# The first two h tiles of the second expert, computed together and copied by token thirds

## The chip, the cores and the metric

The kernel runs on one core of a Trainium2 chip. The metric is device time in microseconds of one execution. The core has a matrix engine (TensorE, PE in the profile, with its weight loads shown apart as PEld), three engines for elementwise work (VectorE = DVE, ScalarE = ACT, GpSimd = POOL) and queues that start transfers between HBM and SBUF, here all from SyncE (SP). PE writes its results to PSUM, from where DVE and ACT read them.

## What is computed

Three blocks follow each other on 1152 tokens (2 x 576) with a model width of 512: attention with rotary positions over 8 heads of 64, a first expert (x wa * x wb) wo of inner width 1536, and a second expert of inner width 2048. The change lies at the start of the second expert:

```python
def _moe2_ref(x, w_in, w_out):
    h = x @ w_in
    g = h - np.tanh(h)
    return (g @ w_out).astype(np.float32)
```

## The kernel before

Every operand of a matmul is split into a high and a low part in a reduced float32 format. `mm3` (lines 188 to 190) makes one product as three matmuls: high x high, high x low, low x high. The tokens are taken in thirds (`t`, TP = 384 columns); the model width in four chunks of 128 (`c`).

The first expert ends with the y units (line 714). For each token third t and each chunk d of the width, PE makes a y tile in PSUM, DVE adds it to yacc (L727), ACT copies the high part of the sum to yt[0] (L735), and POOL subtracts it from the sum for the low part yt[1] (L736). So yt is made chunk by chunk, the last token third last.

The second expert makes 16 h tiles, each of 128 inner columns and all 1152 tokens. `h_unit` (line 781) runs 36 matmuls per tile: 3 thirds x 4 chunks x 3, on the high and low parts of yt. A tile takes three banks of PSUM. There are two pools of one such buffer each: even tiles share one, odd tiles the other, so that tile f + 2 has to wait until the last reader of tile f is done. The odd pool and the pools of the o tiles lie where the last y tiles lay.

Then comes g = h - tanh(h), with a series for small h, on 128 x 1152 elements at a time (the last tile by thirds). ACT makes the square of h (L803), a square with a bias (L806), a mask (L807), tanh (L812) and at the end the high part of g (L818). DVE makes two products (L808, L813), the subtraction h - tanh (L816), a predicated copy that picks one of the two (L817), and the low part of g (L819). The readers of h are L803 and L812 on ACT and L813 and L816 on DVE. For the first two tiles ACT first copies h to the SBUF tile hs (L798); there DVE reads hs, while ACT still reads PSUM. Work buffers are tmpa for even tiles and tmpb for odd ones.

The o units (line 827) multiply g by w2, 12 matmuls for four h tiles and 128 tokens; they begin when the first g tiles are there. Between units, pieces of the weight conversion (lines 120 to 158: a DMA to st, then ACT and DVE steps) are put in with `cv`.

The order on each engine is fixed when the kernel is built: a scheduler lists the instructions of each engine, by the order in the code and by when it expects inputs. At run time each engine goes through its own list in order and waits for counters of the other engines. In the order rows below such a wait stands in brackets with the engine that is waited for; numbers in names are those of buffers.

Of the kernel before, what the change touches and what calls it, by code (L numbers as in the profile page):

```python
# [11 lines left out]
F32 = mybir.dt.float32  # L12
# [6 lines left out]

SIGN_BIT = -2147483648  # L20

# h - tanh(h) = h * u * (1/3 - C1 * u + C2 * u * u), u = h * h, for |h| <= TSMALL
TSMALL = 0.25
C0 = 1.0 / 3.0
C1 = -0.13329779010819712
C2 = 0.052115944387372236
# [3 lines left out]
def attention_moe_kernel(  # L30
# [13 lines left out]
    nc = tc.nc  # L44
# [4 lines left out]
    P = 128  # L49
# [16 lines left out]
        return tc.high_priority(offset=o) if o else nullcontext()  # L66
    PAIRS = [(b, hp) for b in range(B) for hp in range(NPAIR)]

    # ------------------------------------------------------------ pools
    const = ctx.enter_context(tc.tile_pool(name="const", bufs=1))  # L70
    actp = ctx.enter_context(tc.tile_pool(name="actp", bufs=2))
    big = ctx.enter_context(tc.tile_pool(name="big", bufs=2))
# [2 lines left out]
    ident = const.tile([P, P], F32, name="ident")  # L75
    make_identity(nc, ident)

    # ------------------------------------------------------------ float64 weights -> two float32r parts
    units = []
    for f in range(NF1):  # L80
        units.append(("ab", f))
# [130 lines left out]
            r.append(ps)  # L212
        ab_ps[f, t] = r

    # ------------------------------------------------------------ attention
    with ExitStack() as actx:
        ap1 = actx.enter_context(tc.tile_pool(name="ap1", bufs=1))
        ap2 = actx.enter_context(tc.tile_pool(name="ap2", bufs=2))
# [461 lines left out]
        mctx.close()  # L680
        return

    # ------------------------------------------------------------ first expert pair: (x wa * x wb) wo
    slots = ctx.enter_context(tc.tile_pool(name="slots", bufs=12))
    cbuf["slots"] = slots
    wcap[0] = WC1
# [71 lines left out]
            tc.tile_pool(name="ps_or", bufs=1, space=bass.MemoryType.PSUM, side="right")  # L758
        )]

    # ------------------------------------------------------------ second expert: g(y wi) w2
    wcap[0] = WC2
    oacc = big.tile([P, NTT, DM], F32, tag="big", name="oacc")
    cst = const.tile([P, 2], F32, name="cst")
# [8 lines left out]
    with ExitStack():  # L773
        nc.vector.memset(cst[:, 0:1], al)
        nc.vector.memset(cst[:, 1:2], -TSMALL * TSMALL)
        gf = {}
        tmps = [tmpa] + [slots.tile([P, 2, NP3, TP], F32, tag="slot", name="tmpb") for _ in range(NT2 - 1)]
        tht = slots.tile([P, 2, NP3, TP], F32, tag="slot", name="tht") if TM == 0 else None
        hs = slots.tile([P, 2, NP3, TP], F32, tag="slot", name="hs") if NH else None

        def h_unit(f):
            wc = get_w(("i", f // 2)).rearrange("p s (c f) -> p s c f", c=KC)
            ps = ps_h[f % 2].tile([P, NP3, 512], F32, tag="h", name="h")
            o = (f % 2) * P
            for t in range(NP3):
                for c in range(KC):
                    mm3(
                        ps[:, t, 0:TP], lambda s: wc[:, s, c, o:o + P],
                        lambda s: yt[s][:, c, t * TP:(t + 1) * TP], c == 0, c == KC - 1,
                    )  # L790
            g = slots.tile([P, 2, NP3, TP], F32R, tag="slot", name="g")
            ta = tmps[f % NT2]
            last = f == NF2 - 1
            for t in (range(NP3) if last else (slice(0, NP3),)):
                h = ps[:, t, 0:TP]
                if HA <= f < NH:
                    hc = hs[:, f % 2, t]
                    nc.scalar.copy(out=hc, in_=h)  # L798
                else:
                    hc = h  # L800
                u, vv, mk = ta[:, 0, t], ta[:, 1, t], g[:, 0, t]
                th = u if TM else tht[:, f % 2, t]
                nc.scalar.activation(out=u, in_=h, func=AF.Square)  # L803
                if CO and not TM:
                    nc.scalar.activation(out=th, in_=h, func=AF.Tanh)
                nc.scalar.activation(out=vv, in_=u, func=AF.Square, bias=cst[:, 0:1])  # L806
                nc.scalar.activation(out=mk, in_=u, func=AF.Relu, bias=cst[:, 1:2])  # L807
                nc.vector.scalar_tensor_tensor(  # L808
                    out=vv, in0=vv, scalar=de, in1=u, op0=ALU.add, op1=ALU.mult
                )  # L810
                if TM or not CO:
                    nc.scalar.activation(out=th, in_=h, func=AF.Tanh)  # L812
                nc.vector.scalar_tensor_tensor(  # L813
                    out=vv, in0=vv, scalar=C2, in1=hc, op0=ALU.mult, op1=ALU.mult
                )
                nc.vector.tensor_tensor(out=th, in0=hc, in1=th, op=ALU.subtract)  # L816
                nc.vector.copy_predicated(vv, mk.bitcast(U32), th)  # L817
                nc.scalar.copy(out=g[:, 0, t], in_=vv)  # L818
                nc.vector.tensor_tensor(out=g[:, 1, t], in0=vv, in1=g[:, 0, t], op=ALU.subtract)  # L819
            gf[f] = g  # L820
            if f % 2 == 1:
                retire(("i", f // 2))

        GE = 4
        wide = []

        def o_unit(gi, i):
            last = gi == NF2 // GE - 1
            n = i if i < CM else (i - 1 if i > CM else NTT - 1)
            if last and n % 8 not in (3, 7):  # L830
                if n % 4 == 0:
                    wide.append(ps_h[n // 4 % 2].tile([P, NP3, 512], F32, tag="h", name="ow"))
                ps = wide[-1][:, n % 4]
            else:
                ps = ps_o[n // 4 % 2 if last else n % 2].tile([P, DM], F32, tag="o", name="o")
            for n in range(GE):
                f = gi * GE + n
                wc = get_w(("2", f // 2)).rearrange("p s (c d) -> p s c d", c=2)
                if i == CM and f % 2 == 1:
                    retire(("2", f // 2))  # L840
                g = gf[f].rearrange("p s a x -> p s (a x)")
                for m, (a, c) in enumerate(((0, 0), (0, 1), (1, 0))):
                    nc.tensor.matmul(  # L843
                        ps, g[:, a, i * P:(i + 1) * P], wc[:, c, f % 2],
                        start=(n == 0 and m == 0), stop=(n == GE - 1 and m == 2),
                    )
            o = oacc[:, i]
            if gi == 0:
                nc.scalar.copy(out=o, in_=ps)
            else:  # L850
                nc.vector.tensor_tensor(out=o, in0=o, in1=ps, op=ALU.add)
            if last:
                ov = out.rearrange("(b r c) d -> b c r d", b=B, c=CW)
                if i == CM:
                    nc.sync.dma_start(out=out.rearrange("(r c) d -> c r d", c=CW)[CM], in_=o)
                else:
                    for s in range(2):
                        nc.sync.dma_start(out=ov[i // 5, (i if i < CM else i - 5) + 5 * s], in_=o[64 * s:64 * s + 64])

        oq = []  # L860
        for f in range(NF2):
            h_unit(f)
            for _ in range(OE):
                if CHB:
                    cv(CHB)
                if oq:
                    o_unit(*oq.pop(0))
                cv(CH)
            if f % GE == GE - 1:
                oq += [(f // GE, i) for i in (0, 1, 2, 3, 5, 6, 7, 8, 4)]  # L870
            if f >= WG:
                wcap[0] = WCG
        while oq:
            o_unit(*oq.pop(0))
# [45 lines left out]
```

## Time and profile before

| | us |
|---|---|
| runs of the kernel before (3) | 632.22, 631.37, 632.19 |
| their median | 632.19 |
| span of the profiled execution | 632.1 |
| PE busy | 608.2 |
| DVE busy | 481.1 |
| ACT busy | 348.4 |
| POOL busy | 132.4 |

One execution was taken by the profiler, and all durations come from it. No time around its span is given apart from it: the span is the profiled execution's own time, and it agrees with the median of the runs. Attention fills the first 180 us, the first expert ends near 419 us, and the second expert takes the rest. A line as `L190` is line 190 of the kernel before; in the kernel after, the lines of g from the square on (L803) and those of the o units are eight higher.

### The profile page before, as it was taken

To read this page: it belongs to the slowest core of one execution; us is meant where nothing else is said; L and a number is where in the kernel's file an instruction comes from. 1 tells how busy PE (TensorE), PEld (TensorE's weight loads), DVE (VectorE), ACT (ScalarE), POOL (GpSimd) and SP (SyncE) were. 2 spreads that over 40 slices of the span, in tenths; PEclk is the share of its full clock that TensorE was granted. 3 is DMA by queue.
4 is the path that set the end of the run, shared out by engine and by line. 5 is a ranking of instruction groups with operands and counts; after the bars stand their busy time and mean duration, and the time that the engine had idled before them with its cause. 6 is when DMAs were issued, how large, how long until landed. Compare 5 with 4: busy or idle time off the path is not lost.

```text
span 632.1 us, 9300 instructions
## 1 busy us (share of the span) xinstructions
PE 608.2 (96%) x3588; PEld 568.3 (90%) x3588; DVE 481.1 (76%) x646; ACT 348.4 (55%) x579; POOL 132.4 (21%) x121
## 2 busy tenths in 40 slices
PE   7789999999999999999999999998999999999997
PEld 6578988998889999999999999988988988998975
DVE  6868877778788988787757568694976698899572
ACT  2468877787774555533323133356966673585350
POOL 4565877773331000000000000091000000000000
PEclk7789999999999999999999999997999999999999
DMA  3466656753542555534203123320001121310014
GB/s 85 124 157 150 141 131 152 174 127 92 140 153 67 171 166 185 167 111 130 71 8 126 67 67 133 107 94 1 1 1 66 67 66 41 100 60 1 1 40 110
DMA packets 37771, 60.92 MB, mean 96 GB/s; under 512 B 4064, under 2 KB 22496, under 8 KB 37728
## 3 DMA queue, kind: packets, MB, share of 16 engines
q1 hardware_dynamic: 37728, 60.34, 33.3%
q8 instruction: 28, 0.46, 0.3%
q14 instruction: 15, 0.12, 0.1%
HBM read 43.06 MB, written 2.36 MB: 72 GB/s over the span
## 4 chain that ended last, share of the span: by engine, by line
PE 79%; DVE 6%; ACT 6%; POOL 3%; DMA 3%; issue 2%; SPq 1%; POOLq 0%; ACTq 0%; DVEq 0%
PE ab L190 24%; PE h L190 11%; PE o L843 10%; PE y L190 9%; PE acc L500 6%; PE pss L408 6%; PE pst L473 4%; POOL yt L736 3%; PE ow L843 3%; PE psp L362 2%; PE rb L557 2%; ACT st L127 1%; DMA st<-in_moe_w_in_dram 1%; DMA st<-in_moe_w_out_dram 1%; DVE nm L414 1%
## 5 line engine op out<-in xcount | busy, mean ns | idle before, releaser
L190 PE MATMUL ab<-xt,w 128*128 128x384 f32 x504 | 88.6, 334 | 0.5 <-ACT w L152 0.5
L190 PEld LDWEIGHTS ab<-xt,w 128*128 128x128 f32 x504 | 87.4, 188 | 0.8 <-ACT w L152 0.8
L843 PE MATMUL o<-wc,g 128*128 128x512 f32 x348 | 83.8, 392 | 0.4 <-ACT g L818 0.3
L843 PEld LDWEIGHTS o<-wc,g 128*128 128x128 f32 x348 | 64.7, 188 | 14.1 <-ACT g L818 1.3
L190 PE MATMUL y<-g,wc 128*128 128x384 f32 x432 | 76.5, 334 | 0.0
L190 PEld LDWEIGHTS y<-g,wc 128*128 128x128 f32 x432 | 75.0, 188 | 0.0
L408 PE MATMUL pss<-k,q 128*128 128x288 f32 x320 | 64.7, 323 | 2.4 <-ACT p L420 1.3
L414 DVE TENSOR_REDUCE nm<-pss 128x1 f32<-128x576 f32 x72 | 54.0, 753 | 15.9 <-PE pss L408 15.6
L190 PE MATMUL h<-yt,w 128*128 128x384 f32 x360 | 65.4, 335 | 0.1
L190 PEld LDWEIGHTS h<-yt,w 128*128 128x128 f32 x360 | 62.9, 188 | 1.7 <-issue 0.5
L736 POOL TENSOR_TENSOR yt<-yacc,yt 128x384 fp32r<-128x384 f32 x12 | 19.8, 1685 | 207.4 <-ACT yt L735 207.4
L190 PE MATMUL ab<-xt,wc 128*128 128x384 f32 x360 | 63.2, 334 | 0.0
L190 PEld LDWEIGHTS ab<-xt,wc 128*128 128x128 f32 x360 | 62.5, 188 | 0.0
L127 ACT ACTIVATE st<-st 128x1024 f32<-128x1024 f32 x34 | 39.9, 1172 | 35.5 <-DMA st<-in_moe_w_b_dram 16.2
L420 ACT ACTIVATE p<-pss,nm 128x576 f32<-128x576 f32 x72 | 54.0, 750 | 6.6 <-DVE nm L414 6.3
L500 PE MATMUL acc<-ph,v 128*128 128x288 f32 x320 | 55.4, 305 | 0.9 <-ACT ph L478 0.9
L408 PEld LDWEIGHTS pss<-k,q 128*128 128x128 f32 x320 | 47.5, 196 | 7.0 <-ACT p L420 4.3
L480 DVE TENSOR_TENSOR ph<-pst,ph 128x512 fp32r<-128x512 f32 x72 | 48.4, 684 | 4.8 <-ACT ph L478 4.6
L703 ACT COPY tmpa<-ab 128x384 f32<-128x384 f32 x36 | 17.2, 478 | 61.9 <-PE ab L190 61.7
L478 ACT CAST ph<-pst 128x512 fp32r<-128x512 f32 x72 | 42.4, 595 | 10.9 <-PE pst L473 9.5
L500 PEld LDWEIGHTS acc<-ph,v 128*128 128x128 f32 x320 | 45.1, 188 | 2.0 <-issue 1.5
L473 PE MATMUL pst<-ident,p 128*128 128x128 f32 x288 | 45.5, 276 | 1.0 <-DVE ph L480 1.0
(118 smaller groups left out, 1009.1 us busy)
## 6 DMA issues: line engine op xcount, KB each, us to landing
st<-in_moe_w_out_dram SPq DMA_DIRECT2D x14, 1024.0 KB, 4.9
st<-in_moe_w_in_dram SPq DMA_DIRECT2D x8, 1024.0 KB, 5.2
q<-th SPq DMA_DIRECT2D x28, 288.0 KB, 4.9
st<-in_moe_w_a_dram SPq DMA_DIRECT2D x12, 512.0 KB, 3.8
st<-in_moe_w_b_dram SPq DMA_DIRECT2D x12, 512.0 KB, 5.0
k<-th SPq DMA_DIRECT2D x28, 160.0 KB, 2.7
vr<-in_v_dram SPq DMA_DIRECT2D x16, 128.0 KB, 2.9
out_dram<-oacc SPq DMA_DIRECT2D x16, 128.0 KB, 2.4
```

Of the source, the lines that this page charges most:

```text
L127: nc.scalar.activation(out=xs.bitcast(F32), in_=xs.bitcast(F32), func=AF.Copy, scale=2.0 ** -112)
L190: nc.tensor.matmul(ps, w(a), x(c), start=start and n == 0, stop=stop and n == 2)
L408: nc.tensor.matmul(ph[:, a], st, k2[i][:, j, ko + a * HS:ko + (a + 1) * HS], start=(n == 0), stop=(n == len(mms) - 1),)
L414: nc.vector.tensor_reduce(out=nm[:, u:u + 1], in_=ph, axis=AX.XY, op=ALU.max, negate=True)
L420: nc.scalar.activation(out=po.rearrange("p (a x) -> p a x", a=2), in_=ph, func=AF.Exp, bias=nm, scale=1.0, accum_out=sm,)
L473: nc.tensor.transpose(ps[:, t * P:(t + 1) * P], p[:, t, o:o + P], ident)
L478: nc.scalar.copy(out=pu[:, 0, qm(i)], in_=ps)
L480: nc.vector.tensor_tensor(out=pu[:, 1, qm(i)], in0=ps, in1=pu[:, 0, qm(i)], op=ALU.subtract)
L500: nc.tensor.matmul(acc, st, pslot(i, u)[:, s, a * HS:(a + 1) * HS], start=(u == 8 and s == 0), stop=(u == full[-1] and s == 1),)
L703: nc.scalar.copy(out=a[:, t], in_=r[0])
L736: (nc.gpsimd if YLP > d else nc.vector).tensor_tensor(out=yl, in0=o, in1=yh, op=ALU.subtract)
L843: nc.tensor.matmul(ps, g[:, a, i * P:(i + 1) * P], wc[:, c, f % 2], start=(n == 0 and m == 0), stop=(n == GE - 1 and m == 2),)
```

## The change

`h_unit` made one tile at a time, thirds inside. Now a helper `h_mm(f, t)` makes the 12 matmuls of one third of tile f. At f = 0 the first two tiles are made together: third 0 of tile 0, third 0 of tile 1, third 1 of tile 0, and so on. Each third is copied to hs by ACT as soon as it is there: six copies of 128 x 384 in place of two of 128 x 1152. At f = 1 no matmul is made. For these two tiles all of g now reads hs, so that ACT no longer reads their PSUM either. From tile 2 on nothing changes in the code. (The diff also drops some comments.)

```diff
+        h_ps = {}
+
+        def h_mm(f, t):
+            wc = get_w(("i", f // 2)).rearrange("p s (c f) -> p s c f", c=KC)
+            if f not in h_ps:
+                h_ps[f] = ps_h[f % 2].tile([P, NP3, 512], F32, tag="h", name="h")
+            o = (f % 2) * P
+            for c in range(KC):
+                mm3(
+                    h_ps[f][:, t, 0:TP], lambda s: wc[:, s, c, o:o + P],
+                    lambda s: yt[s][:, c, t * TP:(t + 1) * TP], c == 0, c == KC - 1,
+                )
+
         def h_unit(f):
-            wc = get_w(("i", f // 2)).rearrange("p s (c f) -> p s c f", c=KC)
-            ps = ps_h[f % 2].tile([P, NP3, 512], F32, tag="h", name="h")
-            o = (f % 2) * P
-            for t in range(NP3):
-                for c in range(KC):
-                    mm3(
-                        ps[:, t, 0:TP], lambda s: wc[:, s, c, o:o + P],
-                        lambda s: yt[s][:, c, t * TP:(t + 1) * TP], c == 0, c == KC - 1,
-                    )
+            if f == 0:
+                for t in range(NP3):
+                    for n in range(2):
+                        h_mm(n, t)
+                        nc.scalar.copy(out=hs[:, n, t], in_=h_ps[n][:, t, 0:TP])
+            elif f > 1:
+                for t in range(NP3):
+                    h_mm(f, t)
+            ps = h_ps.pop(f)
             g = slots.tile([P, 2, NP3, TP], F32R, tag="slot", name="g")
             ta = tmps[f % NT2]
             last = f == NF2 - 1
             for t in (range(NP3) if last else (slice(0, NP3),)):
-                h = ps[:, t, 0:TP]
-                if HA <= f < NH:
-                    hc = hs[:, f % 2, t]
-                    nc.scalar.copy(out=hc, in_=h)
-                else:
-                    hc = h
+                h = hc = hs[:, f, t] if f < 2 else ps[:, t, 0:TP]
                 u, vv, mk = ta[:, 0, t], ta[:, 1, t], g[:, 0, t]
                 th = u if TM else tht[:, f % 2, t]
                 nc.scalar.activation(out=u, in_=h, func=AF.Square)
```

The scheduler's lists change on PE, ACT and DVE; those of POOL and SP stay as they were. First PE at the seam between the tiles 0 and 1. Before, h_4402 is tile 0 and h_4458 tile 1; these are the last six matmuls of tile 0 and the first of tile 1:

```order
L190 MATMUL h_4402<-yt0_4257,wc_3685 128x384 [waits Activation_49]
L190 MATMUL h_4402<-yt1_4258,wc_3685 128x384 [waits Pool_49]
L190 MATMUL h_4402<-yt0_4257,wc_3685 128x384
L190 MATMUL h_4402<-yt0_4257,wc_3685 128x384 [waits Activation_49]
L190 MATMUL h_4402<-yt1_4258,wc_3685 128x384 [waits Pool_49]
L190 MATMUL h_4402<-yt0_4257,wc_3685 128x384
L190 MATMUL h_4458<-yt0_4257,wc_3685 128x384 [waits DVE_49]
L190 MATMUL h_4458<-yt1_4258,wc_3685 128x384
L190 MATMUL h_4458<-yt0_4257,wc_3685 128x384 x2
```

Now h_4402 is tile 0 and h_4416 tile 1; this is the end of the first third of tile 0, the first third of tile 1, and the start of the second third of tile 0:

```order
L190 MATMUL h_4402<-yt0_4257,wc_3685 128x384
L190 MATMUL h_4416<-yt0_4257,wc_3685 128x384 [waits DVE_49]
L190 MATMUL h_4416<-yt1_4258,wc_3685 128x384
L190 MATMUL h_4416<-yt0_4257,wc_3685 128x384 x2
L190 MATMUL h_4416<-yt1_4258,wc_3685 128x384
L190 MATMUL h_4416<-yt0_4257,wc_3685 128x384 x2
L190 MATMUL h_4416<-yt1_4258,wc_3685 128x384
L190 MATMUL h_4416<-yt0_4257,wc_3685 128x384 x2
L190 MATMUL h_4416<-yt1_4258,wc_3685 128x384
L190 MATMUL h_4416<-yt0_4257,wc_3685 128x384
L190 MATMUL h_4402<-yt0_4257,wc_3685 128x384 [waits Activation_49]
L190 MATMUL h_4402<-yt1_4258,wc_3685 128x384 [waits Pool_49]
```

The first matmul of tile 1 has moved forward by 24 matmuls, with its wait for DVE; a third of tile 0 behind it now waits for ACT (the copy of tile 0's third before) besides POOL.

Then PE in front of tile 4, which takes the PSUM buffer of tile 2. Before, h_4555 is tile 3, h_4603 tile 4, and g_4439 and g_4495 are the g of tiles 0 and 1; three o matmuls on g_4439 stand further up, between tiles 2 and 3:

```order
L190 MATMUL h_4555<-yt0_4257,wc_3761 128x384
L843 MATMUL o_4651<-wc_3973,g_4495 128x512 [waits Activation_49]
L843 MATMUL o_4651<-wc_3973,g_4495 128x512
L843 MATMUL o_4651<-wc_3973,g_4495 128x512 [waits DVE_49]
L843 MATMUL o_4665<-wc_3973,g_4439 128x512 x3
L843 MATMUL o_4665<-wc_3973,g_4495 128x512 x3
L190 MATMUL h_4603<-yt0_4257,w0_2394 128x384 [waits DVE_49,PE_49]
```

Now h_4559 is tile 3, h_4607 tile 4, and g_4482 and g_4500 are the g of tiles 0 and 1:

```order
L190 MATMUL h_4559<-yt0_4257,wc_3761 128x384
L851 MATMUL o_4655<-wc_3973,g_4482 128x512 [waits Activation_49]
L851 MATMUL o_4655<-wc_3973,g_4482 128x512
L851 MATMUL o_4655<-wc_3973,g_4482 128x512 [waits DVE_49]
L851 MATMUL o_4669<-wc_3973,g_4482 128x512 x3
L851 MATMUL o_4655<-wc_3973,g_4500 128x512 [waits Activation_49]
L851 MATMUL o_4655<-wc_3973,g_4500 128x512
L851 MATMUL o_4669<-wc_3973,g_4500 128x512 x2
L851 MATMUL o_4655<-wc_3973,g_4500 128x512 [waits DVE_49]
L851 MATMUL o_4669<-wc_3973,g_4500 128x512
L190 MATMUL h_4607<-yt0_4257,w0_2394 128x384 [waits DVE_49,PE_49]
```

The same 12 o matmuls stand in front of tile 4, but all of them behind tile 3, and tiles 2 and 3 follow each other with nothing between them. The wait of tile 4 for DVE is for L816 (L824 now) on tile 2, the last reader of its buffer.

Last DVE, from the subtraction of tile 0 to that of tile 2. Before (tile 2 is h_4507):

```order
L816 TENSOR_TENSOR tmpa_2520<-hs_4401,tmpa_2520 128x1152 [waits Activation_49]
L817 COPY_PREDICATED tmpa_2520<-g_4439,tmpa_2520 128x1152 [waits DVE_49]
L808 SCALAR_TENSOR_TENSOR tmpb_4400<-tmpb_4400 128x1152 [waits Activation_49]
L819 TENSOR_TENSOR g_4439<-tmpa_2520,g_4439 128x1152 [waits Activation_49]
L813 SCALAR_TENSOR_TENSOR tmpb_4400<-tmpb_4400,hs_4401 128x1152 [waits DVE_49]
L816 TENSOR_TENSOR tmpb_4400<-hs_4401,tmpb_4400 128x1152 [waits Activation_49]
L817 COPY_PREDICATED tmpb_4400<-g_4495,tmpb_4400 128x1152 [waits DVE_49]
L808 SCALAR_TENSOR_TENSOR tmpa_2520<-tmpa_2520 128x1152 [waits Activation_49]
L819 TENSOR_TENSOR g_4495<-tmpb_4400,g_4495 128x1152 [waits Activation_49]
L813 SCALAR_TENSOR_TENSOR tmpa_2520<-tmpa_2520,h_4507 128x1152 [waits PE_49,Activation_49]
L816 TENSOR_TENSOR tmpa_2520<-h_4507,tmpa_2520 128x1152
```

Now (tile 2 is h_4511):

```order
L824 TENSOR_TENSOR tmpa_2520<-hs_4401,tmpa_2520 128x1152 [waits Activation_49]
L816 SCALAR_TENSOR_TENSOR tmpb_4400<-tmpb_4400 128x1152 [waits Activation_49]
L825 COPY_PREDICATED tmpa_2520<-g_4482,tmpa_2520 128x1152 [waits DVE_49]
L821 SCALAR_TENSOR_TENSOR tmpb_4400<-tmpb_4400,hs_4401 128x1152 [waits DVE_49]
L827 TENSOR_TENSOR g_4482<-tmpa_2520,g_4482 128x1152 [waits Activation_49]
L824 TENSOR_TENSOR tmpb_4400<-hs_4401,tmpb_4400 128x1152
L825 COPY_PREDICATED tmpb_4400<-g_4500,tmpb_4400 128x1152 [waits DVE_49]
L816 SCALAR_TENSOR_TENSOR tmpa_2520<-tmpa_2520 128x1152 [waits Activation_49]
L827 TENSOR_TENSOR g_4500<-tmpb_4400,g_4500 128x1152 [waits Activation_49]
L821 SCALAR_TENSOR_TENSOR tmpa_2520<-tmpa_2520,h_4511 128x1152 [waits PE_49,Activation_49]
L824 TENSOR_TENSOR tmpa_2520<-h_4511,tmpa_2520 128x1152
```

The same eleven instructions stand in both. Tile 1's first product (L808, now L816) has moved in front of the predicated copy of tile 0, its second product in front of tile 0's low part. ACT's list changes alike: the square of tile 1 stands in front of tile 0's tanh, and the square of tile 3 in front of tile 2's tanh; before, each stood behind it.

## Rows read from the trace of the kernel before

**Rows 1.** The page, part 1: busy time, share, instructions of the engines.
```profile
PE 608.2 (96%) x3588; PEld 568.3 (90%) x3588; DVE 481.1 (76%) x646; ACT 348.4 (55%) x579; POOL 132.4 (21%) x121
```
**Rows 2.** Waits of PE, 418 to 632: total us, times, longest.
```profile
PE h L190 <- POOL yt L736: 3.2, 4, 1.1
PE ow L843 <- DVE oacc L851: 0.6, 1, 0.6
PE o L843 <- ACT g L818: 0.3, 1, 0.3
```
**Rows 3.** Timeline of PE: start, us, instruction, count, idle before and releaser.
```profile
419.04 4.50 PE L190 MATMUL h<-yt,wc 128*128 128x384 f32 x25
423.91 0.80 PE L190 MATMUL h<-yt,wc 128*128 128x384 f32 x3 [0.37 <-POOL yt L736]
...
427.26 0.88 PE L190 MATMUL h<-yt,wc 128*128 128x384 f32 x3 [1.15 <-POOL yt L736]
429.19 15.61 PE L190 MATMUL h<-yt,wc 128*128 128x384 f32 x74 [1.05 <-POOL yt L736]
...
454.12 6.48 PE L190 MATMUL h<-yt,w 128*128 128x384 f32 x36
```
**Rows 4.** Windows: length, busy us by engine (count), granted clock, DMA, GB/s.
```profile
8.00:18.20 10.20, 9.77 (x41) 7.98 (x42) 7.20 (x15) 3.29 (x8) 6.10 (x4) 0.50 0.24 67
423.50:427.80 4.30, 2.17 (x10) 1.43 (x9) 4.02 (x3) 1.12 (x1) 4.30 (x4) 1.00 0.00 0
429.20:434.60 5.40, 5.40 (x17) 5.40 (x18) 0.90 (x1) 4.33 (x4) 0.00 (x0) 0.50 0.00 0
434.80:444.40 9.60, 9.60 (x57) 9.60 (x56) 6.76 (x6) 6.89 (x8) 0.00 (x0) 1.00 0.00 1
```
**Rows 5.** Chain that ended last: start, us, and what (36 matmuls each).
```profile
472.67 8.20 PE o L843 x36
480.87 6.26 PE h L190 x36
```
**Rows 6.** Timeline of DVE, POOL and ACT around the seam.
```profile
420.84 1.01 DVE L727 TENSOR_TENSOR yacc<-yacc,y 128x384 f32<-128x384 f32 x2
...
409.34 19.79 POOL L736 TENSOR_TENSOR yt<-yacc,yt 128x384 fp32r<-128x384 f32 x12 [207.45 <-ACT yt L735]
...
423.46 1.17 ACT L127 ACTIVATE st<-st 128x1024 f32<-128x1024 f32 x1 [1.06 <-DMA st<-in_moe_w_in_dram]
```
**Rows 7.** Timeline of ACT behind the seam; last a group (busy us, mean ns).
```profile
430.23 1.12 ACT L798 COPY hs<-h 128x1152 f32<-128x1152 f32 x1 [5.61 <-PE h L190]
431.25 1.14 ACT L803 ACTIVATE tmpa<-h 128x1152 f32<-128x1152 f32 x1
432.42 1.26 ACT L806 ACTIVATE tmpa<-tmpa,cst 128x1152 f32<-128x1152 f32 x1
433.58 1.24 ACT L807 ACTIVATE g<-tmpa,cst 128x1152 fp32r<-128x1152 f32 x1
435.16 1.13 ACT L812 ACTIVATE tmpa<-h 128x1152 f32<-128x1152 f32 x1 [0.34 <-DVE tmpa L808]
...
441.95 1.14 ACT L818 CAST g<-tmpa 128x1152 fp32r<-128x1152 f32 x1
...
L703 ACT COPY tmpa<-ab 128x384 f32<-128x384 f32 x36 | 17.2, 478 | 61.9 <-PE ab L190 61.7
```
**Rows 8.** Timeline of DVE behind the seam.
```profile
433.70 1.36 DVE L808 SCALAR_TENSOR_TENSOR tmpa<-tmpa 128x1152 f32<-128x1152 f32 x1 [5.42 <-ACT tmpa L806]
435.10 1.36 DVE L813 SCALAR_TENSOR_TENSOR tmpa<-tmpa,hs 128x1152 f32<-128x1152 f32 x1
...
437.76 1.54 DVE L817 COPY_PREDICATED tmpa<-g,tmpa 128x1152 f32<-128x1152 uint32 x1
...
443.35 1.35 DVE L819 TENSOR_TENSOR g<-tmpa,g 128x1152 fp32r<-128x1152 f32 x1
...
452.62 1.35 DVE L816 TENSOR_TENSOR tmpa<-h,tmpa 128x1152 f32<-128x1152 f32 x1
```

## The prediction

> **What bounds the kernel now.** I read the page first, then the waits of TensorE (PE), then its timeline around the seam between the two experts, then the clock, then ScalarE (ACT) and VectorE (DVE) behind that seam. PE is busy for 96% of a span of 632.1 us [rows 1]: what moves the time is a hole in PE's row, or a stretch at the lower clock. From 418 us on PE loses 3.2 us in four waits for POOL, which makes the low parts of yt (L736), and under 1 us in everything else [rows 2]. The timeline shows the place: h starts at 419.04 with tile 0, runs its first two token thirds, and then has to take the last third at POOL's pace, three matmuls at a time, at 423.91, 425.32 (not shown), 427.26 and 429.19 [rows 3]. A second loss follows. The granted clock was 1.00 up to 427.8, though PE had only 10 matmuls in the last 4.3 us of that; then it was 0.50 (1.2 GHz of 2.4) until 434.6, and after that 1.00 again [rows 4]. From 429.19 to 434.6 PE made 17 matmuls of h at about 0.32 us where the full clock gives 0.174 (6.26 us for 36 [rows 5]): 17 x 0.146 = 2.5 us lost.
>
> Behind the seam PE isn't held back by itself alone. Tile 4 begins at 454.12 [rows 3], right after DVE's subtraction that reads tile 2 ends (452.62 + 1.35 = 453.97 [rows 8]): tiles 2 and 4 share one PSUM buffer. From there to the end PE waits for 0.3 and 0.6 us in all [rows 2], and the steps that appear in the chain of waits in between follow from PE's own work. So I take a shift of tile 4's start, or a loss after it, as a shift of the end, one for one.
>
> **The change at the seam.** No matmul is added: 72 stand in front of tile 2 in both, in another order. Tile 1 now begins after 12 matmuls, 419.04 + 12 x 0.174 = 421.13. But its PSUM buffer still holds the last y tiles, and the order shows its first matmul waiting for DVE. DVE ends the last two yacc additions at 420.84 + 1.01 = 421.85 [rows 6], so PE idles for some 0.8 us, a wait that was hidden before. The other 60 matmuls run from 421.9 to 421.9 + 60 x 0.174 = 432.3. Do they meet POOL? Tile 0's last third starts at 428.2 and reads the last yt chunk from 429.9 on; POOL ends at 409.34 + 19.79 = 429.13 [rows 6]. The POOL waits are gone, and with PE dense no lower clock belongs here. In before tile 1 ended near 438.5 (429.19, then 39 matmuls, 19 of them slow), so the seam itself gives back 6 us.
>
> The thirds bring new waits: a third's first matmul into a buffer waits for ACT's copy of the third before it. The first copy stands behind the last yt casts and is done near 422.9; the second stands behind the conversion at 423.46 + 1.17 = 424.6 [rows 6], which itself waits for a DMA, and is done near 425.1. PE needs them at 424.0 and 426.1, so both cost nothing, with 1 us to spare. If that DMA were late, the copies, PE and everything on ACT would wait with it. Six copies of 0.48 us [rows 7] replace two of 1.12: 0.6 us more on ACT, but four lie in the 5.6 us in which ACT sat idle before 430.23 [rows 7]. That the activations read SBUF and not PSUM I cost at nothing: on DVE a read of hs took 1.36 and one of PSUM h 1.35 [rows 8], and on ACT I bound it at 0 to 0.1 us each, from the square on PSUM (1.14) and the biased one on SBUF (1.26 [rows 7]).
>
> **Where the 6 us go.** Tile 4 needs DVE to be done with tile 2. I follow the new order on ACT and DVE, each step by its duration [rows 7, 8], with 0.09 us of overlap where an instruction needs nothing from the one before it (430.23 + 1.12 against 431.25). Tile 0's last matmul ends near 430.5. ACT: copy, square, biased square, copy of tile 1's last third, mask, square of tile 1, tanh of tile 0: 0.48 + 1.14 + 1.26 + 0.48 + 1.24 + 1.14 + 1.13 = 6.9, less four overlaps, to 437.0. DVE: subtraction, tile 1's first product, predicated copy: 1.35 + 1.36 + 1.54 = 4.25, to 441.2. ACT: cast of g0, 1.14, to 442.4. DVE: low part of g0, tile 1's subtraction, predicated copy, 4.25, to 446.6. ACT: cast of g1, square of tile 3, tanh of tile 2: 3.4 less two overlaps, to 449.9. DVE: product and subtraction of tile 2: 2.7, and some hand-overs, to 452.7. In before the same instruction ended at 453.97, so the two engines give back only 1.3 to 1.4 us. They were already at work at 430.23 on tile 0, and that start hardly moves, since tile 0 still ends with POOL's last chunk.
>
> PE gets there too early. Tiles 2 and 3 fill 432.3 to 444.9 (72 x 0.174). Then six o matmuls (0.228 each [rows 5]) run to 446.2; the next need the cast of g1 (448.0), then its low part on DVE (449.4), and after two more, at 449.9, tile 4 waits until 452.7. Waits of 1.8, 0.5 and 2.8 us: 5.1 us idle of 6.5, for the last 6 us of gain. In before the 12 o matmuls stood in two pieces behind tiles 2 and 3, and no such hole was there.
>
> Without any effect on the clock: 632.1 - 1.4 = 630.7. But this hole is emptier than the one that came before the half clock at 427.8 (10 matmuls in 4.3 us [rows 4]; here 6 o matmuls in the 6.5 us), so I expect the half clock to move from 428 to about 451, and tile 4 to pay for it. By the stretch of before the price is 17 matmuls, 2.5 us; in the likeliest case I take 1.6 to 3.1 (a third less, a quarter more), with 2.3 in the middle. Below it is bounded by 0 (the clock holds), above by the longest half-clock stretch of the trace, 10.2 us at the start [rows 4]: all 36 matmuls of tile 4 at 0.32, 5.3 us. The sum is 632.1 - 1.4 + 2.3 = 633.0. It is made against the profiled execution, whose span of 632.1 lies within 0.1 us of the median of the runs (632.19; 631.37 to 632.22).
>
> The Trainium skill ("TensorE: Matmul & The Clock Gate", section "What's actually happening") puts the lower clock down to an engine that was idle on end. By that rule, read literally, the clock would hold here, as PE's longest wait is 2.8 us with matmuls between, and the time would be 630.7. In this case's trace the clock fell after waits of at most 1.1 us [rows 2, 4], so I go by the row. The page also says that the moment of the switch differs from run to run, which no row here shows.
>
> **The rivals.** (a) The clock holds: 630.7. For it: the matmuls between the waits. Against it: the fall at 427.8 after a milder hole. (b) Slower: the half clock lasts through all of tile 4 and the o matmuls behind it. Price 5.3 us, end 632.1 - 1.4 + 5.3 = 636.0; it passes the line of a measurable loss once more than 18 matmuls of tile 4 run slowly (18 x 0.146 = 2.65). For it: the 10.2 us stretch at the start. Against it: that stretch had holes in it, and tile 4 has none. (c) The gain at the seam goes through to the end: tile 4 starts 6 us sooner and the time is near 626. For it: PE's 96%. Against it: DVE's 453.97 and PE's 454.12. (d) The shift is lost or won elsewhere: a later wait (0.3 us for ACT, 0.6 us for DVE) grows or shrinks by what tile 4 moved, and the end stays at 632.1. For it: the weight conversions behind 490 pass through DMA, ACT and DVE. Against it: they start from PE's release of buffers.
>
> **How the numbers follow.** About 0.2%, 1.3 us, is what a measurement of this kernel can tell from no change: faster is under 630.9, slower over 633.4. The forecast, half clock at tile 4, gets 0.63, from 632.3 to 633.8; two thirds of it lie within the bound (0.42) and the rest above (0.21). (a) 0.14, about two thirds of it faster (0.09). (b) 0.08, slower. (c) 0.04, faster. (d) 0.11, within. Faster 0.13, same 0.58, slower 0.29. The range leaves out (c) and the outer half of (b): 630.4 to 634.8.
>
> **What would show it.** Right: the four waits for POOL gone, one wait of 0.8 us for DVE before tile 1, tile 1 done near 432.3 at a clock of 1.00 throughout; three waits of PE between 446 and 453 for ACT and DVE; tile 4 starting near 452.7, and the clock at 0.50 somewhere between 449 and 459 instead of 428 to 435; tile 5 starting between 462 and 463.5; everything after it shifted by one amount. Wrong: tile 4 starting well before 451 (then ACT and DVE were not the bound), a clock of 1.00 through tile 4, or PE waiting for the copies of the thirds.

## The result and the profile after

The kernel after takes 634.57 us, the median of 7 runs (632.35 to 638.63), against 631.37 for 7 runs of the kernel before (628.22 to 632.22). The medians lie 3.2 us apart; the ratio of the comparison is 1.0066, with a 95% interval of 1.0037 to 1.0094, which is 4.2 us (2.3 to 5.9). So it is slower, by more than the 1.3 us that were taken as the least that can be told. Forecast were 633.0 and no change. 634.57 lies inside the range given, but the forecast's direction was wrong.

The profiled execution of the kernel after has a span of 636.8 us and a time of 638.63, the longest of the seven. First the page (its part 1), answering to [rows 1], and the waits of PE from 410 to 640 us, answering to [rows 2] (total us, times, longest):

```profile
PE 611.5 (96%) x3588; PEld 571.5 (90%) x3588; DVE 482.1 (76%) x646; ACT 348.9 (55%) x583; POOL 131.4 (21%) x121
```
```profile
PE h L190 <- DVE tmpa L824: 2.7, 1, 2.7
PE o L851 <- ACT g L826: 2.4, 3, 1.5
PE h L190 <- DVE yacc L727: 0.6, 1, 0.6
PE ow L851 <- DVE oacc L859: 0.6, 1, 0.6
PE o L851 <- DVE g L827: 0.2, 1, 0.2
```

The four waits for POOL are gone, and new ones for DVE and ACT stand in their place: 3.2 us of POOL against 2.7 + 1.5 + 0.2 us in front of tile 4 and 0.6 in front of tile 1. The timeline of PE, answering to [rows 3], shows where:

```profile
421.61 2.24 PE L190 MATMUL h<-yt,wc 128*128 128x384 f32 x12
424.49 23.17 PE L190 MATMUL h<-yt,wc 128*128 128x384 f32 x132 [0.64 <-DVE yacc L727]
447.50 1.55 PE L851 MATMUL o<-wc,g 128*128 128x512 f32 x6
450.55 1.19 PE L851 MATMUL o<-wc,g 128*128 128x512 f32 x4 [1.50 <-ACT g L826]
451.94 0.73 PE L851 MATMUL o<-wc,g 128*128 128x512 f32 x2 [0.20 <-DVE g L827]
455.35 9.18 PE L190 MATMUL h<-yt,w 128*128 128x384 f32 x36 [2.68 <-DVE tmpa L824]
```

h starts 2.57 us later than in the first trace (421.61 against 419.04), and that was lost in attention and the first expert, ahead of the change. So from here on I count from h's start. Tiles 0 to 3 are one dense row of 144 matmuls. Then come the three waits of the prediction, and tile 4 starts 33.74 us behind h's start (the prediction's 452.7 is 33.66). But it takes 9.18 us, not 6.48. The windows (columns as in [rows 4]) say why:

```profile
421.60:447.00 25.40, 24.76 (x143) 24.44 (x143) 19.80 (x17) 17.91 (x22) 9.09 (x6) 1.00 0.14 42
447.00:454.30 7.30, 3.97 (x16) 2.41 (x14) 6.57 (x6) 6.50 (x7) 0.00 (x0) 1.00 0.00 0
454.50:461.10 6.60, 5.75 (x18) 5.78 (x19) 6.60 (x6) 2.62 (x3) 0.00 (x0) 0.50 0.00 0
461.30:480.00 18.70, 18.70 (x95) 16.62 (x94) 11.41 (x10) 11.99 (x13) 0.00 (x0) 1.00 0.01 2
```

The half clock has moved from the seam to tile 4. DVE and ACT, answering to [rows 6 to 8]: tile 0's last copy, the first product, and the subtraction that lets tile 4 go, with POOL's low parts.

```profile
411.90 18.79 POOL L736 TENSOR_TENSOR yt<-yacc,yt 128x384 fp32r<-128x384 f32 x12 [207.47 <-ACT yt L735]
...
433.14 0.48 ACT L799 COPY hs<-h 128x384 f32<-128x384 f32 x1 [1.60 <-PE h L190]
433.65 1.17 ACT L811 ACTIVATE tmpa<-hs 128x1152 f32<-128x1152 f32 x1
...
436.14 1.36 DVE L816 SCALAR_TENSOR_TENSOR tmpa<-tmpa 128x1152 f32<-128x1152 f32 x1 [4.37 <-ACT tmpa L814]
...
453.85 1.35 DVE L824 TENSOR_TENSOR tmpa<-h,tmpa 128x1152 f32<-128x1152 f32 x1
```

POOL ends at 430.69, 9.08 us behind h's start; tile 0's copy waits for PE and comes at 11.53. So up to here the mechanism is the one that was predicted, with one exception: tile 0's end is set by PE's new order and no longer by POOL. What is not explained is the size. From h's start to the start of the last 36 o matmuls this execution takes 202.44 us (624.05 - 421.61) and the first trace of before 200.33: 2.1 us more, where the runs say 3.2 (their medians) to 4.2 (their ratio).

### The profile page after: what moved, and what is told of

Read it like the earlier page. It is cut to its first block, busy times and chain, and to the rows that moved or that the text cites. A ratio compares the mean times of both kernels' runs of the same rounds, so it can differ in the third digit from the quotient of the medians.

```text
span 636.8 us, 9300 instructions
## 1 busy us (share of the span) xinstructions
PE 611.5 (96%) x3588; PEld 571.5 (90%) x3588; DVE 482.1 (76%) x646; ACT 348.9 (55%) x583; POOL 131.4 (21%) x121
## 4 chain that ended last, share of the span: by engine, by line
PE 77%; DVE 11%; ACT 6%; DMA 3%; issue 2%; SPq 1%; POOL 0%; DVEq 0%; ACTq 0%; POOLq 0%
PE ab L190 24%; PE y L190 11%; PE o L851 10%; PE h L190 9%; PE acc L500 6%; PE pss L408 6%; PE pst L473 4%; PE ow L851 3%; PE rb L557 2%; PE psp L362 2%; DMA st<-in_moe_w_out_dram 1%; DVE st L135 1%; DVE tmpa L824 1%; DMA st<-in_moe_w_in_dram 1%; DVE wc L154 1%
## 5 line engine op out<-in xcount | busy, mean ns | idle before, releaser
L190 PE MATMUL h<-yt,w 128*128 128x384 f32 x360 | 68.2, 345 | 2.7 <-DVE tmpa L824 2.7
L190 PEld LDWEIGHTS h<-yt,w 128*128 128x128 f32 x360 | 65.5, 195 | 4.6 <-issue 3.5
L408 PE MATMUL pss<-k,q 128*128 128x288 f32 x320 | 66.1, 328 | 2.0 <-ACT p L420 0.8
```

The costliest lines, as they stand in the source:

```text
L190: nc.tensor.matmul(ps, w(a), x(c), start=start and n == 0, stop=stop and n == 2)
L408: nc.tensor.matmul(ph[:, a], st, k2[i][:, j, ko + a * HS:ko + (a + 1) * HS], start=(n == 0), stop=(n == len(mms) - 1),)
```

## The experiments

Two theories went in. A: the profiled execution of before was a bad one, its half clock at the seam is not there in every run, and against a usual run the change loses twice, by a later tile 4 and by its half clock. B: the base was right, and the loss stands somewhere else. All times are medians. The runs were made in three comparisons, each with the kernel before beside them, at 631.30 us (33 runs; with it both kernels again, the filled hole and the filled waits), 630.91 (29; tile 0 first, the order alone, the control of the filled waits) and 630.85 (35; the kernels with a tile of zeros alone, and the filled waits again). A ratio is against the kernel before of the same comparison, with its 95% interval.

### Both kernels again

The kernel before, unchanged:

> The kernel before, unchanged, profiled a second time. Theory A (the base was a disturbed execution): the half clock behind the waits for POOL at the seam is not there in every execution. Here the profile shows either a granted clock of 1.00 from the first to the fourth h tile with tile 4 starting some 32.5 us behind h's start (35.1 in the first trace), or the fall again; over its runs the time spreads by 2 to 4 us, and the shorter ones show the higher mean clock. Theory B (the base was right, the loss is somewhere else): the fall at the seam again, tile 4 at 35.1 +- 0.2 us behind h's start. Both: a median of 630 to 632.5, ratio 0.998 to 1.002.

> The kernel before, profiled a third time, to see how the seam differs from execution to execution. Theory A: the length of the half clock at the seam (6.8 us in the first trace, 3.4 in the second) and of POOL's 12 subtractions (19.8 and 18.6 us) again differ or equal one of the two, and tile 4's start behind h's start follows them (35.1 and 32.9 us). Theory B: the first trace is the rule: 6.8 us, 19.8 us, 35.1 us.

The kernel after, unchanged:

> The kernel after, unchanged, profiled a second time. Theory A: the hole in front of tile 4 drops the clock in nearly every execution, so tile 4's 36 matmuls take 8 to 9.5 us again (6.3 at full clock) and the runs lie near 634.5; tile 4 starts 33.7 us behind h's start. Theory B: tile 4's length differs from execution to execution and doesn't go with the time; the loss of 4 us against before shows up behind tile 5. Both: ratio 1.004 to 1.009.

Measured: 631.78 (ratio 0.9984, 0.9960 to 1.0007) for before; for its third profile one time, 629.52; for after 634.66 (1.0031, 1.0004 to 1.0059). The timelines of PE in the second and the third execution of before:

```profile
416.95 5.02 PE L190 MATMUL h<-yt,wc 128*128 128x384 f32 x28
422.69 0.79 PE L190 MATMUL h<-yt,wc 128*128 128x384 f32 x3 [0.72 <-POOL yt L736]
424.10 0.79 PE L190 MATMUL h<-yt,wc 128*128 128x384 f32 x3 [0.62 <-POOL yt L736]
426.03 14.49 PE L190 MATMUL h<-yt,wc 128*128 128x384 f32 x74 [1.14 <-POOL yt L736]
...
449.85 6.50 PE L190 MATMUL h<-yt,w 128*128 128x384 f32 x36
```
```profile
418.10 5.54 PE L190 MATMUL h<-yt,wc 128*128 128x384 f32 x31
424.72 0.79 PE L190 MATMUL h<-yt,wc 128*128 128x384 f32 x3 [1.08 <-POOL yt L736]
426.12 13.32 PE L190 MATMUL h<-yt,wc 128*128 128x384 f32 x74 [0.61 <-POOL yt L736]
...
448.56 6.50 PE L190 MATMUL h<-yt,w 128*128 128x384 f32 x36
```

Four waits for POOL in the first trace [rows 3], three here, then two; 74 matmuls in 15.61, 14.49 and 13.32 us. The clock in windows at the seam, of the second and the third execution:

```profile
425.80:429.20 3.40, 3.17 (x10) 3.17 (x11) 1.26 (x1) 2.12 (x2) 0.18 (x1) 0.52 0.00 0
429.20:434.00 4.80, 4.80 (x30) 4.80 (x29) 3.41 (x3) 3.57 (x4) 0.00 (x0) 1.00 0.01 2
```
```profile
422.00:426.60 4.60, 2.91 (x16) 2.27 (x15) 4.50 (x3) 1.50 (x2) 4.07 (x3) 1.00 0.08 32
426.60:432.00 5.40, 5.40 (x33) 5.40 (x32) 3.48 (x4) 4.85 (x5) 0.00 (x0) 1.00 0.00 0
```

The half clock lasted 6.8 us in the first, 3.4 in the second, and did not come at all in the third. This table has the profiled executions of these and the following kernels, in us behind h's start (P is the time from the start to the end of POOL's 12 subtractions, ½ the length of the half clock at the seam or at tile 4, in the order alone at tile 2, and L what PE waits in all between 130 and 150 us behind h's start, of which more below):

| execution | P | ½ | tile 0's last copy starts | tile 4 starts | its 36 matmuls | last 36 o start | L |
|---|---|---|---|---|---|---|---|
| before, first | 19.79 | 6.8 | 11.19 | 35.08 | 6.48 | 200.33 | 0 |
| before, second | 18.62 | 3.4 | 10.13 | 32.90 | 6.50 | 200.08 | 1.74 |
| before, third | 17.44 | 0 | 8.68 | 30.46 | 6.50 | 196.82 | 0.91 |
| after, first | 18.79 | 6.8 | 11.53 | 33.74 | 9.18 | 202.44 | 0.66 |
| after, second | 18.90 | 6.8 | 11.61 | 33.83 | 9.13 | 202.89 | 1.02 |
| after, hole filled | 18.59 | 0 | 11.50 | 33.74 | 6.48 | 199.12 | 0 |
| after, tile 0 first | 18.66 | 0 | 9.77 | 31.01 | 6.48 | 198.11 | 1.64 |
| the same, zero tile | 17.62 | 0 | 10.53 | 31.76 | 6.48 | 197.59 | 0.68 |
| after, zero tile | 18.70 | 6.8 | 11.50 | 33.71 | 9.08 | 203.67 | 1.85 |
| before, zero tile | 18.72 | 3.4 | 10.12 | 32.97 | 6.48 | 199.94 | 1.57 |
| order alone | 18.58 | 3.4 | 11.53 | 36.52 | 6.50 | 203.33 | 1.41 |
| before, waits filled | 17.62 | 0 | 9.64 | 31.41 | full clock | 196.66 | 0 |
| the same, again | 18.71 | 0 | 9.78 | 31.57 | full clock | 196.74 | 0 |
| before, same fill elsewhere | 17.32 | 3.4 | 8.64 | 34.70 | full clock | 199.77 | 0 |

Tile 4's start in before runs from 30.5 to 35.1 with the same program; in the profiled executions of after it is 33.7 to 33.8 each time, and each time tile 4 has the half clock. That is theory A's picture, and the first trace was its far end. POOL's pace alone does not settle whether the half clock comes at the seam: 17.44 went with none, 17.32 (the last row) with 3.4 us of it.

### The hole in front of tile 4 filled

`zr` is a tile of zeros that is made at the start (shown further down). Sixteen matmuls on it are added to the o tile (cut):

```diff
                         start=(n == 0 and m == 0), stop=(n == GE - 1 and m == 2),
                     )
+                if (gi, i) == (0, 1):
+                    for _ in range((6, 10, 0, 0)[n]):
+                        nc.tensor.matmul(ps, zr, wc[:, 0, f % 2], start=False, stop=False)
```

> The kernel after with 16 matmuls on a tile of zeros added to the second o tile in front of tile 4 (6 behind the products of g0, 10 behind those of g1): they add nothing to the sums and fill most of PE's hole. Theory A: the clock stays at 1.00 through tile 4 (6.3 us instead of 9.2), tile 4 starts where it did, 33.7 to 34 us behind h's start, and the time falls by 1.6 to 3 us from the kernel after, to 631.5 to 633; it stays above the fast executions of the kernel before (628 to 629). Theory B (the half clock at tile 4 costs nothing in the end, later waits take it up): within 0.7 us of the kernel after, near 634.5.

Measured: 631.69 (0.9992, 0.9967 to 1.0016), 3.0 us under the kernel after in the same comparison. The timeline of PE (L861 are the added ones), and the window over the former hole and the one over tile 4:

```profile
449.13 2.49 PE L861 MATMUL o<-wc,zr 128*128 128x512 f32 x10
451.97 6.48 PE L194 MATMUL h<-yt,w 128*128 128x384 f32 x36 [0.35 <-DVE tmpa L828]
```
```profile
445.20:451.90 6.70, 6.07 (x24) 3.98 (x23) 6.01 (x6) 5.49 (x5) 0.00 (x0) 1.00 0.00 0
452.00:458.30 6.30, 6.30 (x37) 6.30 (x38) 6.30 (x5) 2.30 (x2) 0.00 (x0) 1.00 0.00 0
```

Tile 4 starts where it did and runs at full clock: 9.13 (the second execution of after) - 6.48 = 2.65 us of the 3.0 are shown directly. The 16 added matmuls do nothing for the sums; they only keep PE busy.

### Tile 0's second and last thirds moved up

In after the thirds come as 0.0, 1.0, 0.1, 1.1, 0.2, 1.2 (tile.third). Here two pairs of neighbours are swapped: 0.0, 0.1, 1.0, 0.2, 1.1, 1.2, so that tile 0's last third stands behind 36 matmuls and not 48.

```diff
-                for t in range(NP3):
-                    for n in range(2):
-                        h_mm(n, t)
-                        nc.scalar.copy(out=hs[:, n, t], in_=h_ps[n][:, t, 0:TP])
+                for n, t in ((0, 0), (0, 1), (1, 0), (0, 2), (1, 1), (1, 2)):
+                    h_mm(n, t)
+                    nc.scalar.copy(out=hs[:, n, t], in_=h_ps[n][:, t, 0:TP])
```

> The kernel after with one thing undone: the order of the six thirds is 0.0, 0.1, 1.0, 0.2, 1.1, 1.2 (tile.third), so tile 0's last third stands behind 36 matmuls and not 48. Theory A (after loses twice: tile 0's end stands behind tile 1's thirds, and the hole in front of tile 4 brings the half clock): tile 0's last copy starts near 10.2 us behind h's start (11.5 in after), tile 4 near 32 us (33.8 in after), its 36 matmuls take 6.4 us because the hole is smaller (three waits of 0.5 to 0.9 us), time 629.5 to 631.5. Theory B (tile 0's delay costs nothing, only the clock matters): tile 4 stays at 33.7, time 632 to 634.7.

Measured: 630.53 (0.9990, 0.9966 to 1.0015), 4.1 us under after's 634.66 of the first comparison, where the kernel before was 0.4 us slower than in this one. From the timelines of ACT and PE, tile 0's last copy and tile 4:

```profile
429.49 0.48 ACT L798 COPY hs<-h 128x384 f32<-128x384 f32 x1 [1.70 <-PE h L190]
...
449.37 0.73 PE L850 MATMUL o<-wc,g 128*128 128x512 f32 x2 [0.20 <-DVE g L826]
450.73 6.48 PE L190 MATMUL h<-yt,w 128*128 128x384 f32 x36 [0.63 <-DVE tmpa L823]
```

The copy comes 9.77 us behind h's start instead of 11.5, tile 4 at 31.01 instead of 33.8, and PE's waits in front of it shrink to 0.25, 0.20 and 0.63, and the clock holds. Two swapped pairs in an order of six are the difference between losing 3 to 4 us and being even with before.

### The order alone

The matmuls stay interleaved as in after, but each tile is copied once and whole, and ACT reads h in PSUM again (cut):

```diff
                         h_mm(n, t)
-                        nc.scalar.copy(out=hs[:, n, t], in_=h_ps[n][:, t, 0:TP])
 ...
-                h = hc = hs[:, f, t] if f < 2 else ps[:, t, 0:TP]
+                h = hc = ps[:, t, 0:TP]
+                if f < 2:
+                    hc = hs[:, f, t]
+                    nc.scalar.copy(out=hc, in_=h)
```

> The kernel after without the copies by thirds: the matmuls of the first two tiles interleaved, but one copy of 128 x 1152 per tile, and ACT reads h in PSUM as before. Theory A: tile 2 must wait for tile 0's tanh, which now ends behind both tiles' matmuls: PE idles 5 to 6 us in front of tile 2 and 2 us in front of tile 4, tile 4 starts near 36.5 us behind h's start, the half clock comes in at tile 2 (2.5 us) and maybe at tile 4: 636 to 640. Theory B (the order alone is what pays, the copies cost): 631 to 634.

Measured: 635.02 (1.0065, 1.0038 to 1.0091), 1 us under what A gave and 1 us above B's range. PE in front of tile 2:

```profile
437.42 2.93 PE L190 MATMUL h<-yt,wc 128*128 128x384 f32 x8 [5.54 <-ACT tmpa L822]
```

Tile 2 waits 5.54 us for tile 0's tanh, which reads PSUM. The half clock came behind it for 3.4 us, and tile 4's wait was 0.54, not 2: A's 36.5 for tile 4 holds, and tile 4 ran at full clock, so its price for the clock was too high. The copies by thirds bring tile 4 forward by 2.8 us (33.8), but the half clock then falls on tile 4, and in time nothing is left that can be told: 635.02 here, 634.57 and 634.66 for after in other comparisons. With the copies and without them this order loses.

### The waits for POOL filled, in the kernel before

The three matmuls of `mm3` are written out, and 18 on the tile of zeros are put in behind the first of them (cut; the first line is of the new form, too):

```diff
                     nc.tensor.matmul(hp_, w[0], x[0], start=c == 0, stop=False)
+                    if (f, t) == (0, 2):
+                        for _ in range((2, 4, 6, 6)[c]):
+                            nc.tensor.matmul(hp_, zr, x[0], start=False, stop=False)
```

> The kernel before with 18 matmuls on a tile of zeros put into the four waits for POOL at the seam (2, 4, 6, 6), so that PE has less idle time there. Theory A: no half clock at the seam; tile 1 ends and ACT, DVE and tile 4 follow as in an execution without the fall: tile 4 about 32.5 us behind h's start, the time 628.5 to 630, 1 to 2.5 us under the median of the kernel before, with less spread. Theory B: no gain, since tile 4 waits for DVE in any case: 631 to 632.5. If the added matmuls themselves delay the low parts (they cannot pass the waits in front of them), 632 to 633.

> The kernel before with the 18 matmuls on zeros in the waits for POOL, unchanged, a second time. If its gain is real: 628.2 to 629.5, 1.5 to 3 us under the kernel before, no half clock at the seam, tile 4 some 31 to 32 us behind h's start. If the first job had luck with the executions: 630 to 631.

The control, the same 18 in one block in tile 1's last third (`(f, t, c) == (1, 2, 2)`):

> The kernel before with the 18 matmuls on zeros not in the waits for POOL, but in one block in tile 1's last third (3.1 us of PE at full clock). If the filled waits are what made the other kernel faster, this one gains nothing: tile 4 comes some 1 to 1.5 us later than in an execution of before without them (33.5 to 36 us behind h's start), the half clock at the seam stays as often as in before, and the time is 632 to 635. If the added matmuls help wherever they stand: 628.5 to 630.

Measured: 628.66 (0.9955, 0.9929 to 0.9980) and 628.92 (0.9978, 0.9954 to 1.0002); the control 633.21 (1.0032, 1.0004 to 1.0060). So the added matmuls gain where they fill waits and lose where they stand in PE's dense row. The window over the filled stretch, of the first of the two, and the block of the control:

```profile
424.00:429.20 5.20, 5.20 (x32) 5.20 (x31) 5.06 (x4) 1.16 (x1) 3.71 (x3) 1.00 0.02 8
```
```profile
435.69 3.35 PE L797 MATMUL h<-yt,zr 128*128 128x384 f32 x18
```

This is the fastest kernel of the study, 1.9 to 2.6 us under the kernel before beside it, though the second interval just reaches 1. Its medians lie under those of both kernels in every comparison. Not all of the gain is seen at the seam: tile 4 starts at 31.4 and 31.6, some 1.4 us before the average of the four executions of before in the table (32.85), and 1 us behind the best of them, which had no half clock to lose. The rest, about 1.2 us at the last 36 o matmuls (196.7 against 199.3), arises behind tile 4, where these executions have none of the waits L.

### The tile of zeros alone

```diff
+    zf = const.tile([P, P], F32, name="zf")
+    nc.vector.memset(zf, 0.0)
+    zr = const.tile([P, P], F32R, name="zr")
+    nc.vector.tensor_copy(out=zr, in_=zf)
```

> A control: the kernel after with the tile of zeros made at the start (a memset and a copy of 128 x 128 on DVE, and 64 KB more of SBUF for each of the two tiles) but no matmul on it. In the traces so far the transfer of second-expert weights some 135 to 140 us behind h's start lands 0.9 to 2 us late in the kernels without this tile and in none with it. If the tile alone is what changed that, the waits near 145 to 149 us (0.3 to 1 us in all) go away here too and the time is 633.3 to 634.3; if it is chance, 634 to 635. In both cases the half clock at tile 4 stays (9.1 us for its 36 matmuls), so the 3 us of the filled hole are not to be had by the tile alone: more than 632.8.

> The same control on the kernel before: the tile of zeros, no matmul on it. If the 2.6 us of the kernel with filled waits came from the waits (POOL's pace covered and PE kept busy), this one lies within 1 us of the kernel before, 630.2 to 631.8, and the waits for POOL and the half clock at the seam are there in some executions. If they came from the tile (addresses, the late transfer), 628.5 to 629.5.

> The kernel after with tile 0's last third moved up (order 0.0, 0.1, 1.0, 0.2, 1.1, 1.2), with the tile of zeros and no matmul on it. If the late transfer goes with the tile, the 1.6 us of waits near 140 to 144 us behind h's start disappear: 628.5 to 630. If it is chance: 630.5 as without the tile. Tile 4 at 31 us behind h's start and 6.5 us long in both.

Measured: 634.49 (1.0054, 1.0024 to 1.0084), 632.51 (1.0019, 0.9989 to 1.0049) and 630.25 (0.9983, 0.9958 to 1.0009): the tile by itself gains nothing on either kernel (the second is 0.7 above what was expected at most, with an interval that holds 1). The order with tile 0 first is again even with before, and it is 4.2 us under after with the same tile in the same comparison (630.25 against 634.49), where the order is all that differs; tile 4 came at 31.76 and not at 31, since PE's wait for yacc was 1.49 us in this execution. What I had suspected, that the tile keeps the transfer of second-expert weights from landing late, is wrong: DVE waited for it in all three again, by 2.15, 1.90 and 0.86 us. Here is that wait in the third of them, then in the first, and PE's two waits behind it in the first, which make its L of 1.85 us:

```profile
551.41 0.70 DVE L132 TENSOR_SCALAR st<-st 128x1024 int32<-128x1024 int32 x1 [0.86 <-DMA st<-in_moe_w_out_dram]
```
```profile
557.88 0.70 DVE L132 TENSOR_SCALAR st<-st 128x1024 int32<-128x1024 int32 x1 [2.15 <-DMA st<-in_moe_w_out_dram]
```
```profile
562.39 1.80 PE L194 MATMUL h<-yt,w 128*128 128x384 f32 x9 [1.17 <-DVE tmpb L828]
...
566.08 1.21 PE L855 MATMUL o<-wc,g 128*128 128x512 f32 x4 [0.68 <-ACT g L830]
```

The table shows a pattern that no experiment here takes apart: L is 0 in all four executions with added matmuls on zeros, the control among them, and 0.66 to 1.85 us in nine of the ten without. It may be chance, or the added matmuls may change when that transfer lands. What decides it stays open, and with it how much of the gains of the filled hole and of the filled waits comes from there; L averages 1.2 us in the three executions of after and 1.1 in the four of before, and about that much is the most it can be, as an estimate. Tile 4 in the first (33.71 behind h's start) had the half clock once more:

```profile
450.39 9.08 PE L194 MATMUL h<-yt,w 128*128 128x384 f32 x36 [2.67 <-DVE tmpa L828]
```

## Why the prediction was wrong

**The step that failed: the base.** Of its sum the prediction says: "It is made against the profiled execution, whose span of 632.1 lies within 0.1 us of the median of the runs". Two things were wrong in that. The time of an execution is 1.8 to 1.9 us more than its span: 631.61 against 629.8, 635.02 against 633.2, and so in each run that lists both. A span that equals the median of the times is therefore no sign of a usual execution, as the prediction and the section on the time before took it to be: the one that was profiled took about 634, above all the runs shown (631.37 to 632.22). And its seam was the worst of three executions of the same program: 6.8 us of half clock where the others had 3.4 and none, 19.79 us for POOL where they had 18.62 and 17.44. The sum set off its 2.5 us of half clock and its slow POOL as if they were part of the kernel in every execution.

**The term that fell with it: the 1.4 us by which tile 4 was to start earlier.** The time after was right: 33.7 to 33.8 behind h's start, 33.66 forecast. The time before was not: with the control of before on the zero tile (32.97) the four executions average 32.85, so where the sum has -1.4 the change moves tile 4 back by 0.9 us on average, and by 3.3 against the best. The four spread over 4.6 us, so the 0.9 is good to about 1 us (an estimate from that spread).

**"That start hardly moves, since tile 0 still ends with POOL's last chunk."** True only beside a POOL of 19.79. Tile 0's last third stands behind 48 matmuls now, and its copy starts 11.5 us behind h's start in all four traces with this order and the copies by thirds, held by PE and not by POOL (P 18.59 to 18.90); in before it followed POOL, from 8.7 to 11.2. The order with tile 0 first shows the price: tile 4 at 31.01 and 31.76 instead of 33.8.

**The half clock moving to tile 4, at 2.3 us (1.6 to 3.1).** Right in place, and the size within its bounds: 9.13 on average against 6.49, 2.64 us, in three executions out of three (the filled hole gives it back). Rival (a), that the clock holds, fell: the clock went to 0.50 behind waits of 1.50, 0.20 and 2.68 us with matmuls between. The rule of the Trainium skill ("TensorE: Matmul & The Clock Gate", "What's actually happening"), read literally, would have had it hold, and these rows go against it as those of before did. The three executions of before differed at one place of one program, by 6.8, 3.4 and 0 us of half clock. The same section of the Trainium skill says that the moment of the switch differs from run to run, of the start of a kernel; it should have been a warning.

**The sum made again.** 0.9 + 2.64 = 3.5 us, and the last 36 o matmuls start 202.99 us behind h's start in after (three executions) against 199.29 in before (four): 3.7. The medians of the runs lie 3.2 us apart in the result and 3.4 where both kernels were run again. With the base at 631.4, the same terms give 634.9 for the 634.57 measured; so close an agreement is more than four executions of before can promise. And that 633.0 came within 1.6 us was in part luck: tile 4's start was wrong by 2.3 us, and a base 0.7 us above the median of the runs made up for some of it.

**The rest.** Right: PE's wait of 0.8 for yacc (0.64 and 0.73 in after), the thirds' copies at no cost, no half clock at the seam, three waits in front of tile 4 (1.8, 0.5, 2.8 forecast; 1.50, 0.20, 2.68). Rival (d) is there at the rim: a wait for ACT near 148 us behind h's start took 0.66 in after, but in the second trace of before it was there too (0.69), so it is not the change's. Rivals (b) and (c) fell: only the first part of tile 4 was slow, and nothing of the 6 us at the seam came through.

## What to carry to other kernels

Before a change is set off against a profiled execution, ask which of its losses every execution has: compare its time with the runs, and take a half-clock stretch or a wait with a varying length as a range, not as an amount that the change removes. When two tiles are interleaved to hide a slow producer, the first tile must not end later for it if the engines behind PE are the bound: put in only as many matmuls as the waits hold. A gap in front of a dense stretch can cost the gap and then the clock: here it did so in three executions out of three.

## What the chip showed

- POOL's 12 subtractions took 17.44, 18.62 and 19.79 us in three executions of one program: steps of about 1.17. The rows of DVE beside them go with it. In the third execution and in the first (L135 once in 2.08 us and once in 1.21):

```profile
414.41 1.57 DVE L128 TENSOR_SCALAR st<-st 128x1024 int32<-128x1024 int32 x1
...
421.71 2.08 DVE L135 SCALAR_TENSOR_TENSOR st<-st 128x1024 int32<-128x1024 int32 x1
```
```profile
415.34 0.68 DVE L128 TENSOR_SCALAR st<-st 128x1024 int32<-128x1024 int32 x1
...
421.77 1.21 DVE L135 SCALAR_TENSOR_TENSOR st<-st 128x1024 int32<-128x1024 int32 x1
```

  Where DVE's conversion steps ran slowly, POOL was quick; in the second execution one of the two was quick (L128, 0.68), and POOL took one step of 1.17 more. The Trainium skill ("SBUF — State Buffer", "SBUF: two separate sides") says that the two engines share a pair of ports that one instruction holds to its end while the other stands still. These rows fit that; no experiment took one of the engines away, so the cause is not shown.
- In the 97 runs of before beside the experiments, the granted clock over a whole execution lay between 0.975 and 1.000, and the time between 626.67 (0.997) and 637.98 us (0.977). In the traces the half-clock stretches ahead of the second expert lie within the first 45 us and near 180 to 188 us, and differ from execution to execution.
- A transfer of w_out for the second expert kept DVE waiting for 0.96 us in the first trace of after and 2.03 in the second of before, and not in the first of before; so it comes and goes with no edit. Where it was late, PE waited 0.66 to 1.85 us behind it.
